# Raw weights of the first column pair loaded before the last expert matrices, into freed token rows, in a fused attention, mixture and feed-forward kernel

## The chip, the cores and the metric

The kernel runs on one core of a Trainium2 chip. The metric is the device time of one execution in microseconds (us), as the median over several runs. Engine names in the profile: PE (TensorE matmul), PEld (TensorE weight load), DVE (VectorE), ACT (ScalarE), POOL (GpSimd), SP (SyncE, which issues all DMAs here; SPq is its queue).

## The reference

Three stages follow each other; all data is float32.

```python
# 1. attention, B=2, H=8, S=768, D=64: keys within 16 of the query, and one summary per block of 32
k_sum = k.reshape(B, H, 24, 32, D).max(axis=3);  v_sum = v.reshape(B, H, 24, 32, D).mean(axis=3)
a = softmax(concat(mask(scale * q @ k.T), scale * q @ k_sum.T + log(32)))
x = (a @ concat(v, v_sum)).reshape(1536, 512)
# 2. soft mixture, 8 experts with 4 slots each, F=1024
logits = x @ phi
slot_in = softmax(logits, axis=0).T @ x                  # "dispatch": 32 slots, 512
slot_out[e] = relu(slot_in[e] @ w1[e]) @ w2[e]           # w1: 8 x 512 x 1024, w2: 8 x 1024 x 512
y = softmax(logits, axis=1) @ slot_out
# 3. feed-forward, 512 -> 2048 -> 512
out = softplus(y @ w_in) @ w_out
```

The inputs are 60 MB, of which w1 and w2 are 16.8 MB each and w_in and w_out 4.2 MB each.

## The kernel before, in words

All work is cut into named tasks (`task`, L171), and two lists written out by hand, `ORDER_A` (L65, attention and dispatch) and `ORDER_B` (L18, experts and feed-forward), say in which order they are emitted (`run`, L174). Each engine executes its own instructions in that order and waits for others by semaphores; so one list sets the order within PE, DVE, ACT, POOL and within the queue of DMA issues on SP. A DMA whose target is still in use holds up all that stand behind it on SP. `warm n` (L650) emits n bf16 filler matmuls on PE.

**Memory.** Ten slots `s0` to `s9` of 16 KB per partition (L138) hold first q, k and v of the four head groups, then w1 (`W1`, L185), then w2 (`W2`, L186: expert 0 in s0, 1 in s1, 2 in the softmax buffer `AB`, 3 to 7 in s6, s7, s8, s9, s2), then the raw words of w_in (s3, s5, s2, s3) and w_out (s4, s6, s9, s4). So w2 of experts 3 to 7 can be sent only when the matmuls that read w1 in that slot are through. The tokens x (the output of attention, `x`, L163) are two tiles of 6 x 512 words per partition; from L657 on their place is given to other pools, among them `wt_p` with two buffers of 4 KB under the tag "wo" and `ep`.

**Attention** (12 steps i of 4 windows, 3 per head group g): `k`, `q`, `v` load; `km` (L251, DVE) takes block maxima; `kf` (L258, POOL) copies keys and maxima into windows; `vp`, `ve` (ACT) copy shifted v rows; `va` to `vd` (PE, ACT) form the block means, and `vf` (`fill_v`, L296, POOL) copies them into rows 96 to 119 of v of both strips (a strip is one of the two alignments of v) for two chunks at once. Then `sc` (PE), `mx`, `sub` (DVE), `ex` (ACT), `tr` (PE), `tc` (ACT), `av` (PE), `dv` (DVE). Dispatch: `xt`, `lt`, `lm`, then `sp` (L474) and `zp` (L518), the last matmuls that read x.

**Experts:** `hu E n` (L785): up projection of experts 2E and 2E+1, half n of the rows of w1, on PE; `hr` (relu, ACT, L796), `ht` (transpose, PE, L801), `hc` (DVE, L806); `dn e h` (L810): down projection of expert e, half h of w2[e], PE; `so` (ACT) collects all but `dn 7 1`, which `yl 0`, `yl 1` (L819) make by themselves; `ya` (L825, DVE) adds, `yt` (PE), `ye` (ACT, DVE) give the transposed slot outputs `soT`. Beside it `c 0` to `c 6`, `ct`, `cc` prepare the combine weights.

**Feed-forward:** w_in and w_out are read as float64-like word pairs and put together: `wia`/`woa` (L712, ACT) rescale the high word, `wib`/`wob` n (n = 0, 1, 2: L718, L720, L723, DVE) shift and merge the fields. They are done in eight pairs p (256 columns of w_in, two rows blocks of w_out); pair 0 is halved (`wia 0 0`, `wia 0 1`). `wh`, `wl` (ACT, DVE) split w_out into a high and a low part. `swc`, `swd`, `swe` (L906, L912, L915) multiply w_in with the slot outputs into `SW`. A visit is 128 columns of the hidden layer for half of the tokens: `ha` (L918, PE), `hx` (softplus, ACT, L931), `hh`, `hl` (high and low part; ACT, DVE), `m` (L943, 18 matmuls per visit into six accumulators); there are 32 visits. `leave` and `out` bring results out.

Loads of raw w_in before: `wi 0 0 0` and `wi 0 0 1` (`load_wi`, L221) are the two column halves of pair 0, all four k, in rows of 1 KB, into s3.

Of the kernel before, what the change touches and what calls it, by code (L numbers as in the profile page):

```python
# [28 lines left out]
m 1 1 1, swd 1:ACT, hl 1, swe 1, wob 1 2, m 1 0 1, woa 2, m 1 1 0, ha 2, m 1 2 1, m 1 0 0, m 1 2 0, wib 2 2, hx 2,  # L29
hh 2, wob 2 0, wh 1, swa 2, m 2 0 0, swb 2:ACT, wia 3, ha 3, hl 2, hx 3, wob 2 1, wl 1:DVE, wob 2 2, hh 3, m 2 0 1,  # L30
m 2 2 1, swc 2, m 2 2 0, m 2 1 1, m 3 0 1, swd 2:DVE, wib 3 0, swe 2, ha 4, wib 3 1, wib 3 2, wo 1 1, wi 2 0, hl 3,
wh 2, woa 3, hx 4, m 2 1 0, m 3 1 1, wob 3 0, wia 4, m 3 0 0, wl 2:DVE, hh 4, swa 3, wib 4 0, swb 3:ACT, m 3 2 1,
ha 5, wo 2 0, swc 3, hl 4, swd 3:ACT, wi 3 1, m 3 1 0, m 4 0 0, hx 5, wo 2 1, m 4 1 0, wob 3 1, m 4 2 1, swe 3,
wob 3 2, woa 5, m 4 1 1, hh 5, ha 6, m 4 2 0, wib 4 1, hl 5, hx 6, m 5 1 1, wh 3, ha 7, hh 6, m 5 0 1, wi 2 1,
m 3 2 0, hx 7, m 6 0 1, ha 8, wia 5, wob 5 0, m 4 0 1, hl 6, hh 7, wib 4 2, m 5 1 0, wl 3:DVE, wia 7, swa 4, hx 8,
m 6 1 1, wib 5 0, swb 4:ACT, m 6 1 0, m 6 0 0, wob 5 1, ha 9, wib 5 1, m 6 2 1, hl 7, m 5 2 1, wi 3 0, wia 6, hx 9,
hh 8, wib 6 0, m 7 4, m 6 2 0, wib 5 2, m 7 3, swc 4, wib 7 0, leave 7 4:ACT, woa 4, m 5 0 0, m 5 2 0, hl 8,
swd 4:ACT, m 7 5, hh 9, wob 5 2, m 7 2, swe 4, ha 10, swa 5, swb 5:ACT, wob 4 0, wib 6 1, wo 3 0, hx 10, wib 7 1,
m 8 4, leave 7 5:DVE, m 7 1, ha 11, wh 5, wob 4 1, leave 7 1:DVE, leave 7 3:DVE, m 7 0, hl 9, wib 6 2, hh 10,
leave 7 0:ACT, m 8 0, swc 5, hl 10, m 8 1, hx 11, m 8 5, leave 7 2:ACT, m 8 2, swd 5:ACT, swe 5, m 8 3, ha 12, swa 6,  # L40
hh 11, wl 5:DVE, m 9 0 1, m 10 1 1, m 11 0 0, woa 6, m 9 1 0, swb 6:ACT, m 10 1 0, hl 11, hx 12, m 9 2 1, m 9 0 0,
ha 13, wob 6 0, m 10 2 1, swc 6, swd 6:DVE, m 11 0 1, wib 7 2, wob 6 1, hx 13, m 10 0 1, m 10 0 0, wob 4 2, m 9 1 1,
wo 3 1, hh 13, m 9 2 0, m 13 0 1, m 13 1 0, swe 6, ha 14, m 11 1 1, swa 7, wh 4, hh 12, m 10 2 0, hl 13, m 13 2 1,
wl 4:DVE, swb 7:ACT, m 11 2 1, hx 14, wob 6 2, ha 15, hl 12, woa 7, m 13 0 0, swc 7, m 12 1 1, m 11 2 0, wob 7 0,
wob 7 1, m 13 1 1, swd 7:DVE, hh 14, m 13 2 0, m 11 1 0, hx 15, hh 15, m 12 2 0, m 12 0 0, m 12 2 1, swe 7, m 14 1 1,
ha 16, m 15 1 1, wh 6, m 14 1 0, hl 15, hx 16, ha 17, m 15 0 0, m 14 0 1, m 12 0 1, m 15 2 1, m 15 0 1, hl 14,
m 15 1 0, hx 17, wob 7 2, hh 16, ha 18, hl 16, m 15 2 0, m 14 0 0, m 12 1 0, hx 18, m 14 2 1, m 16 1 1, m 16 0 1,
hh 17, hl 17, wl 6:DVE, m 16 2 1, m 16 1 0, hh 18, m 16 2 0, ha 19, m 16 0 0, m 17 2 0, hl 18, m 18 0 0, m 17 0 1,
hx 19, ha 20, m 18 2 1, hh 19, m 19 0 1, m 19 1 0, m 17 2 1, hx 20, m 18 1 1, m 18 2 0, m 17 0 0, wh 7, m 14 2 0,
hl 19, m 17 1 0, m 18 1 0, ha 21, m 17 1 1, m 19 1 1, m 19 0 0, hx 21, ha 22, hh 20, m 18 0 1, hl 20, wl 7:DVE,  # L50
m 20 1 0, m 20 0 0, hh 21, hx 22, ha 23, m 20 2 1, m 20 2 0, hh 22, m 21 0 1, m 19 2 0, hl 22, m 22 1 0, m 21 1 0,
m 20 1 1, hl 21, hx 23, ha 24, m 20 0 1, m 21 2 0, m 21 0 0, m 19 2 1, hh 23, hx 24, m 21 1 1, m 22 1 1, ha 25,
m 22 0 1, m 22 2 1, hl 23, hx 25, m 21 2 1, ha 26, m 22 2 0, m 23 4, m 23 5, hh 24, leave 23 5:DVE, m 22 0 0, hl 24,
m 23 2, m 23 1, leave 23 1:DVE, hx 26, m 23 0, hh 25, ha 27, m 23 3, m 24 0, leave 23 4:ACT, m 24 4, m 24 1, hh 26,
hl 25, leave 23 3:DVE, leave 23 2:ACT, m 24 5, m 24 2, hx 27, hl 26, ha 28, leave 23 0:ACT, m 24 3, m 25 1 0,
out 23 1, hh 27, out 23 5, hx 28, m 25 1 1, m 25 0 0, m 25 0 1, hh 28, m 26 1 1, m 25 2 1, hl 28, out 23 4, ha 29,
m 28 0 0, m 26 0 0, m 28 1 0, hx 29, m 28 1 1, m 26 2 1, m 28 0 1, m 27 0 1, m 25 2 0, ha 30, m 28 2 0, m 26 0 1,
m 26 1 0, hl 27, out 23 0, m 26 2 0, hx 30, hh 29, hh 30, m 27 2 0, hl 29, m 29 0 0, m 27 0 0, m 29 1 1, m 27 2 1,
# [7 lines left out]
k 0 0, k 1 0, km 0 0, km 1 0, warm 28, q 0 0, kf 0 0 0:Pool, k 0 1, km 0 1, bias, kf 0 0 1:Pool, kf 1 0 2:Pool, q 0 1,  # L66
kf 0 1 0:Pool, kf 1 0 1:Pool, v 0 0, sc 0, v 0 1, va 0, ve 0 0:ACT, mx 0, k 1 1, q 1 1, sub 0, v 1 0, ve 0 1:ACT,
kf 0 0 2:Pool, kf 0 1 1:Pool, kf 1 0 0:Pool, vb 0:ACT, km 1 1, sc 1, kf 0 1 2:Pool, q 1 0, vp 0 1:ACT, sc 2, ex 0 0,
v 2 0, k 2 0, v 2 1, mx 1, kf 1 1 0:Pool, sub 1, ex 0 1, kf 1 1 1:Pool, vp 0 0:ACT, tr 0 0, tc 0 0:ACT, vc 0, tr 0 1,
vd 0:ACT, vf 0 1:Pool, v 1 1, vf 0 0:Pool, k 2 1, ex 1 0, mx 2, sc 3, sub 2, ex 1 1, tc 0 1:ACT, ve 2 0:ACT, km 2 0,  # L70
tr 1 1, kf 2 0 0:Pool, ex 2 1, tc 1 1:ACT, ex 2 0, vp 1 1:ACT, av 0 0, av 0 1, mx 3, tr 1 0, sc 4, dv 0, tr 2 1, mx 4,
k 3 1, kf 2 0 2:Pool, kf 1 1 2:Pool, tc 1 0:ACT, km 2 1, tc 2 1:ACT, q 2 1, k 3 0, sub 3, va 1, av 1 0, ve 0 2:ACT,
vb 1:ACT, vc 1, ve 2 2:ACT, q 2 0, vp 2 1:ACT, vf 0 2:Pool, w1 3 0, vd 1:ACT, km 3 1, vp 1 0:ACT, kf 2 0 1:Pool,
av 1 1, tr 2 0, ve 2 1:ACT, tc 2 0:DVE, vp 2 0:ACT, ex 3 0, kf 2 1 0:Pool, va 2, kf 2 1 1:Pool, sc 5, phi, ve 1 0:ACT,
vf 1 0:Pool, sub 4, sc 6, dv 1, km 3 0, av 2 1, ex 3 1, mx 5, kf 3 0 0:Pool, av 2 0, ve 1 1:ACT, q 3 1, dv 2, tr 3 0,
vb 2:ACT, ex 4 0, ex 4 1, tr 3 1, sub 5, vf 1 1:Pool, kf 2 1 2:Pool, mx 6, tc 3 0:ACT, w1 1 0, tc 3 1:ACT, vc 2,
ve 1 2:ACT, av 3 1, av 3 0, tr 4 1, kf 3 0 2:Pool, vd 2:ACT, tr 4 0, ex 5 1, sc 7, dv 3, w1 2 1, tc 4 0:ACT, sub 6,
# [949 lines left out]
```

## Time and profile before

| what | us |
|---|---|
| median of 3 runs (290.81 to 291.77) | 290.92 |
| the profiled execution | 291.39 |
| its span in the trace (1.69 lies around it) | 289.7 |
| busy in the span: PE, DVE, ACT, POOL | 274.7, 161.0, 143.1, 33.9 |
| attention and dispatch, to the first up projection | 0 to 85.45 |
| experts, to the last down projection | 85.45 to 119.8 |
| first hidden tile (`ha 0`) | 125.96 |

The times in the trace count from the start of the span. In lists of instructions each line has start, duration, engine, source line, operation, out<-in, count, and in brackets how long the engine was idle before it and what ended that. A run of PE matmuls is pipelined; its pace is read from the starts, not from the durations.

### The profile page before, as it was taken

The numbers are of one execution on the slowest core, as the hardware profiler recorded it, in microseconds if no ns is written. First come the engines' busy times: TensorE is split into PE (matmuls) and PEld (weight loads), VectorE is DVE, ScalarE is ACT, GpSimd is POOL, SyncE is SP. The second block draws the span as 40 slices with busy tenths as digits, with TensorE's granted clock in tenths as the row PEclk, the third lists the DMA queues.
The fourth block names the chain that finished last, engine by engine and source line by source line (L and its number), as shares of the span: only waits on it lengthen the run. The fifth ranks groups of instructions, "written<-read, shape, count | busy, mean of one in ns | idle before, by whom it ended". The sixth has DMA issues, their size and how long they took to land.

```text
span 289.7 us, 5589 instructions
## 1 busy us (share of the span) xinstructions
PE 274.7 (95%) x2340; PEld 191.3 (66%) x2340; DVE 161.0 (56%) x249; ACT 143.1 (49%) x219; POOL 33.9 (12%) x79
## 2 busy tenths in 40 slices
...
DVE  2598978642654030499999999394342221611224
...
GB/s 232 411 409 402 353 417 424 413 425 417 372 292 286 371 422 423 388 399 397 395 395 298 2 1 2 0 0 0 2 0 0 0 2 0 109 111 0 0 0 217
DMA packets 17432, 63.65 MB, mean 220 GB/s; under 512 B 1920, under 2 KB 3072, under 8 KB 13312
## 3 DMA queue, kind: packets, MB, share of 16 engines
...
q8 instruction: 18, 0.29, 0.4%
q14 instruction: 6, 0.05, 0.0%
...
## 4 chain that ended last, share of the span: by engine, by line
PE 57%; DVE 16%; DMA 12%; ACT 8%; issue 4%; SPq 1%; POOL 1%; DVEq 0%; ACTq 0%; POOLq 0%
PE acc L949 36%; DMA wo_raw<-in_moe_w_out 6%; PE av L358 3%; ACT s L166 3%; PE f_ps L923 3%; DMA s<-in_moe_w 3%; PE h_ps L790 3%; DMA s<-in_v 3%; DVE wf L720 2%; DVE gl L768 2%; PE tpa L342 2%; ACT AB L337 2%; DVE wo L720 2%; DVE wf L723 2%; PE tpx L380 2%
## 5 line engine op out<-in xcount | busy, mean ns | idle before, releaser
L949 PE MATMUL acc<-whl,gh 128*128 128x512 f32 x384 | 105.5, 399 | 0.2
L949 PEld LDWEIGHTS acc<-whl,gh 128*128 128x128 f32 x384 | 71.1, 188 | 17.1 <-ACT park L166 0.7
L768 DVE TENSOR_TENSOR gl<-e,gh 128x768 fp32r<-128x768 f32 (+1 forms) x33 | 30.6, 930 | 49.7 <-ACT gh L166 26.3
L949 PE MATMUL acc<-whl,gl 128*128 128x512 f32 x192 | 58.1, 398 | 0.0
L931 ACT ACTIVATE e<-f_ps 128x768 f32<-128x768 f32 (+1 forms) x33 | 26.0, 789 | 42.5 <-PE f_ps L923 21.8
L949 PEld LDWEIGHTS acc<-whl,gl 128*128 128x128 f32 x192 | 35.8, 188 | 8.5 <-DVE gl L768 0.6
L166 ACT ACTIVATE gh<-e 128x768 fp32r<-128x768 f32 (+1 forms) x33 | 27.0, 824 | 24.3 <-PE acc L949 24.0
L166 ACT ACTIVATE s<-s 32x520 f32<-32x520 f32 (+4 forms) x20 | 14.4, 721 | 9.8 <-DMA s<-in_v 9.4
L923 PE MATMUL f_ps<-cs 128*128 128x384 f32 x64 | 16.9, 345 | 1.4 <-DVE cs L768 1.1
L358 PE MATMUL av<-s,AB 120*64 120x65 f32 x384 | 15.7, 226 | 1.3 <-POOL s L249 0.7
L358 PEld LDWEIGHTS av<-s,AB 120*64 120x64 f32 x384 | 13.0, 137 | 5.9 <-issue 3.2
L342 PE MATMUL tpa<-ident,AB 128*120 128x128 f32 x96 | 14.8, 283 | 1.3 <-ACT vs L166 0.5
L249 POOL COPY s<-vs 24x1040 f32<-24x1040 f32 x12 | 12.6, 1053 | 29.3 <-issue 15.3
L923 PEld LDWEIGHTS f_ps<-cs 128*128 128x128 f32 x64 | 11.6, 188 | 5.9 <-DVE cs L768 1.1
L166 ACT ACTIVATE AB<-tpa 120x512 f32<-120x512 f32 x23 | 13.3, 591 | 4.1 <-PE tpa L342 4.0
L325 DVE TENSOR_REDUCE m<-sc 128x8 f32<-128x960 f32 x12 | 13.8, 1150 | 2.5 <-PE sc L320 2.5
L332 DVE TENSOR_TENSOR AB<-sc,m 128x960 f32<-128x960 f32 x12 | 13.8, 1152 | 2.3 <-PE tpa L342 2.1
L337 ACT ACTIVATE AB<-AB 128x480 f32<-128x480 f32 x24 | 13.6, 598 | 1.1 <-DVE AB L332 0.9
L812 PE MATMUL so_ps<-s,hT 128*32 128x512 f32 x104 | 12.4, 597 | 1.8 <-DMA s<-in_moe_w 1.8
L790 PE MATMUL h_ps<-s,siT 128*32 128x512 f32 x128 | 13.9, 593 | 0.0
L342 PEld LDWEIGHTS tpa<-ident,AB 128*120 128x120 f32 x96 | 10.1, 137 | 4.2 <-ACT vs L166 1.2
L320 PE MATMUL sc<-s 64*64 64x120 f32 x384 | 12.1, 263 | 0.5 <-DMA s<-in_q 0.5
(148 smaller groups left out, 310.8 us busy)
## 6 DMA issues: line engine op xcount, KB each, us to landing
s<-in_moe_w SPq DMA_DIRECT2D x30, 1024.0 KB, 12.5
wi_raw<-in_moe_w_in SPq DMA_DIRECT2D x7, 1024.0 KB, 15.3
...
```

Source lines behind the costliest of these rows:

```text
L166: nc.scalar.activation(out=o, in_=i, func=ACTF.Copy)
L249: (nc.vector if eng == "DVE" else nc.gpsimd).tensor_copy(out=o, in_=i)
L325: nc.vector.tensor_reduce(out=m.rearrange("p (e u) -> p e u", e=2), in_=sc_t[i][:, :, 0:480].rearrange("p e (u j) -> p e u j", u=4), axis= ...
L332: nc.vector.tensor_tensor(out=A_t[i], in0=sc_t[i][:, :, 0:480].rearrange("p e (u j) -> p e u j", u=4), in1=m_t[i].rearrange("p (e u) -> p ...
L337: nc.scalar.activation(out=A_t[i][:, e], in_=A_t[i][:, e], func=ACTF.Exp, scale=0.125)
L342: nc.tensor.transpose(tp[0:120, u], A_t[i][:, e, u, :], ident)
L358: mm(out=av_t[i][64 * w:64 * w + 64, e, 65 * u:65 * u + 65], lhsT=AT_t[i][0:120, e, c:c + 64], rhs=v_t[g][0:120, w, 2 * n + t, 2 * a + e, ...
L768: (nc.vector if eng == "DVE" else nc.gpsimd).tensor_tensor(out=o, in0=i, in1=h.bitcast(F32), op=ALU.subtract)
L790: mm(out=h_ps[E][32 * j:32 * j + 32], lhsT=siT[:, kk], rhs=w1_t[2 * E + j // 2, n][:, kk % 2, 512 * (j % 2):512 * (j % 2) + 512], start=(k ...
L923: mm(out=f[n][:, h, 0:384], lhsT=cs_t["SW"][:, J], rhs=cs_t["cS"][:, s0:s0 + 384], **one)
L931: nc.scalar.activation(out=e_[n][:, half(hs)], in_=f[n][:, half(hs), 0:384], func=ACTF.Softplus)
L949: mm(out=acc[(n > 7) + (n > 23), t], lhsT=g, rhs=(wh, wl, wh)[p][J], start=(n in OPEN and p == 0), stop=(n in SHUT and p == 2))
```

## The change

Four edits:
1. `load_wi0` takes the place of `load_wi` for pair 0: `wi 0 0 a` loads k rows 2a and 2a+1 of all 256 columns, in rows of 2 KB, into a tile of `wt_p` with the tag "wo". `wi_parts` cuts pair 0 by k instead of by columns; the instructions of `wia 0 *`, `wib 0 * n` keep their size.
2. `fill_v` copies one strip per call, 24 x 520 words instead of 24 x 1040; there are 24 calls instead of 12.
3. The softmax scalars of `c 0` and `c 2` move to a tile of their own (`cms`), and `cs` grows by 256 words.
4. Both orders are new.

```diff
+    cms = cp.tile([128, 24], F32, name="cms")
...
+    raw0 = {}
+    def load_wi0(a):
+        raw0[a] = wt_p.tile([128, 2, 256, 2], I32, tag="wo", name="raw0")
+        nc.sync.dma_start(
+            out=raw0[a].rearrange("p k f w -> p k (f w)"),
+            in_=w_in.bitcast(I32).rearrange("(k p) f -> p k f", k=4)[:, 2 * a:2 * a + 2, 0:512])
...
-    def fill_v(g, n, eng):
-        o = v_t[g][96:120, :, 2 * n:2 * n + 2].rearrange("p s c h d -> p s c (h d)")
-        m = vs_t[g][96:120].rearrange("p h d -> p (h d)").unsqueeze(1).unsqueeze(1)
-        on(eng, o, m.to_broadcast([24, 2, 2, 260]))
+    def fill_v(g, n, s, eng):
+        o = v_t[g][96:120, s, 2 * n:2 * n + 2].rearrange("p c h d -> p c (h d)")
+        on(eng, o, vs_t[g][96:120].rearrange("p h d -> p (h d)").unsqueeze(1).to_broadcast([24, 2, 260]))
...
-    cs = cs_p.tile([128, 3584], FR, name="cs")
+    cs = cs_p.tile([128, 3840], FR, name="cs")
...
-            t = ep.tile([128, 1560], F32, name="cw")
-            cs_t["m"], cs_t["s"] = t[:, 0:12].unsqueeze(2), t[:, 12:24].unsqueeze(2)
+            t = ep.tile([128, 1536], F32, name="cw")
+            cs_t["m"], cs_t["s"] = cms[:, 0:12].unsqueeze(2), cms[:, 12:24].unsqueeze(2)
...
+        if p == 0:
+            ks = slice(2 * j[0], 2 * j[0] + 2)
+            return wf_t[0][:, ks, 0:256], raw0[j[0]][:, :, :, 1], raw0[j[0]][:, :, :, 0]
...
-            task(("wi", c, h) + j, P(load_wi, c, ("s3", "s5", "s2", "s3")[c], h, *j))
+            task(("wi", c, h) + j, P(load_wi0, *j) if p == 0 else P(load_wi, c, ("s3", "s5", "s2", "s3")[c], h, *j))
```

The start of ORDER_B, to the second visit (`ha 1`) and a little on:

```diff
-warm 2, c 0, hu 1 0, hu 1 1, c 1, hu 0 0, c 2, hu 2 0, hu 2 1, w2 5 0, hu 0 1, c 4, hu 3 0, c 3, hu 3 1, c 6, c 5,
-hr 0, ct 1, w2 5 1, warm 2, w2 7 0, wi 0 0 0, w2 3 0, ht 0, w2 4 0, w2 4 1, warm 2, hr 1, hc 0 1, hc 0 0, ct 0, ht 1,
-hc 1 0, cc 1, dn 0 0, hr 2, ht 2, dn 0 1, hc 2 1, cc 0, hr 3, hc 2 0, ht 3, dn 5 0, w2 6 1, hc 3 0, dn 1 1, wia 0 0,
-w2 6 0, dn 2 0, wib 0 0 0, dn 2 1, hc 1 1, dn 5 1, dn 4 1, hc 3 1, w2 3 1, w2 7 1, dn 4 0, dn 3 0, dn 1 0, dn 6 0,
-dn 3 1, dn 6 1, dn 7 0, wib 0 0 1, wo 0 0 0, yl 1, so, wib 0 0 2, wo 0 0 1, yl 0, woa 0 0, ya 1, wi 0 0 1, woa 0 1,
-warm 2, ya 0, wob 0 0 0, yt 1, wi 0 1, wo 0 1, ct 2, warm 2, yt 0, wob 0 0 1, ye 0:ACT, warm 2, wob 0 1 0, wob 0 0 2,
-fp, warm 2, warm 2, wia 0 1, wob 0 1 1, ye 1:DVE, swc 0 0, wib 0 1 0, wh 0 0, wob 0 1 2, cc 2, swd 0 0:ACT, wib 0 1 1,
-wia 1, warm 2, swe 0 0, warm 2, ha 0, wib 0 1 2, wi 1 0, hx 0 0, wl 0 0:DVE, swc 0 1, wib 1 0, hh 0 0, hl 0 0,
-wib 1 1, hx 0 1, hh 0 1, m 0 0, wh 0 1, m 0 1, hl 0 1, woa 1, m 0 2, wib 1 2, swd 0 1:DVE, wo 1 0, wob 1 0, swe 0 1,
-m 0 3, wl 0 1:DVE, wia 2, swa 1, swb 1:ACT, ha 1, m 0 5, wi 1 1, hx 1, m 0 4, hh 1, swc 1, wib 2 0, wob 1 1, wib 2 1,
+c 0, c 1, warm 2, wi 0 0 1, hu 2 0, hu 2 1, wi 0 0 0, hu 1 0, hu 0 0, hu 0 1, hu 3 0, hr 0, w2 7 0, hu 1 1, warm 2,
+ht 0, warm 2, c 2, warm 2, c 4, hr 1, w2 7 1, hc 0 0, dn 0 0, w2 6 0, ht 1, w2 5 0, dn 0 1, w2 3 1, hu 3 1, wia 0 0,
+warm 2, hc 1 0, warm 2, c 3, hc 0 1, c 5, w2 4 0, w2 4 1, hr 2, wib 0 0 0, w2 5 1, ht 2, c 6, hr 3, dn 2 0, hc 1 1,
+wia 0 1, w2 6 1, hc 2 0, hc 2 1, dn 1 0, ht 3, hc 3 1, ct 0, w2 3 0, dn 5 0, dn 4 0, cc 0, ct 2, wo 0 0 0, dn 1 1,
+warm 2, ct 1, cc 1, hc 3 0, dn 4 1, wib 0 1 0, wo 0 0 1, dn 2 1, dn 5 1, wi 0 1, wib 0 0 1, wib 0 1 1, wi 1 0, dn 6 1,
+dn 6 0, wo 0 1, dn 3 1, wib 0 0 2, dn 3 0, dn 7 0, woa 0 0, yl 0, wib 0 1 2, wob 0 0 0, so, yl 1, wob 0 0 1, ya 0,
+yt 0, warm 2, woa 0 1, ya 1, cc 2, wob 0 1 0, wob 0 0 2, ye 0:ACT, yt 1, fp, wob 0 1 1, wh 0 0, ye 1:DVE, swc 0 0,
+wob 0 1 2, wia 1, wib 1 0, warm 2, warm 2, swd 0 0:ACT, wi 1 1, swe 0 0, ha 0, swc 0 1, wh 0 1, wl 0 0:DVE, hx 0 0,
+hh 0 0, hx 0 1, hh 0 1, wl 0 1:DVE, wo 1 0, wo 1 1, hl 0 0, m 0 2, m 0 0, wib 1 1, wi 2 1, hl 0 1, wia 2, woa 1,
+wib 1 2, m 0 4, m 0 5, swd 0 1:DVE, swe 0 1, swa 1, swb 1:ACT, wob 1 0, ha 1, m 0 1, hx 1, m 0 3, wob 1 1, hh 1,
...
```

The start of ORDER_A (the rest holds the same tasks in another order, with `vf g n s` for `vf g n`):

```diff
-k 0 0, k 1 0, km 0 0, km 1 0, warm 28, q 0 0, kf 0 0 0:Pool, k 0 1, km 0 1, bias, kf 0 0 1:Pool, kf 1 0 2:Pool, q 0 1,
-kf 0 1 0:Pool, kf 1 0 1:Pool, v 0 0, sc 0, v 0 1, va 0, ve 0 0:ACT, mx 0, k 1 1, q 1 1, sub 0, v 1 0, ve 0 1:ACT,
+k 0 1, km 0 1, bias, k 0 0, q 0 1, q 0 0, k 1 0, km 0 0, kf 0 0 2:Pool, v 0 0, kf 0 0 1:Pool, warm 28, ve 0 0:ACT,
+kf 0 0 0:Pool, kf 0 1 1:Pool, km 1 0, sc 1, kf 0 1 0:Pool, vp 0 0:ACT, v 0 1, sc 0, va 0, kf 1 0 1:Pool, k 1 1, q 1 0,
+kf 1 0 0:Pool, q 1 1, mx 1, v 2 0, vb 0:ACT, mx 0, ve 0 2:ACT, kf 0 1 2:Pool, sub 0, vc 0, vd 0:ACT, ex 0 1, sc 2,
...
```

## Rows read from the trace of the kernel before

**Rows 1.** The page's forty slices of the span, 7.24 us each

```profile
DVE  2598978642654030499999999394342221611224
...
GB/s 232 411 409 402 353 417 424 413 425 417 372 292 286 371 422 423 388 399 397 395 395 298 2 1 2 0 0 0 2 0 0 0 2 0 109 111 0 0 0 217
```

**Rows 2.** Busy time by stretch: length, then PE, PEld, DVE, ACT, POOL, granted clock, DMA

```profile
12.00:24.00 12.00, 10.97 (x221) 7.68 (x223) 11.32 (x15) 11.35 (x19) 6.90 (x17) 1.00 1.04 414
24.00:36.00 12.00, 10.79 (x208) 7.86 (x210) 11.06 (x21) 10.84 (x20) 8.60 (x17) 1.00 0.98 367
...
84.50:88.40 3.90, 3.90 (x46) 1.45 (x48) 2.62 (x7) 1.81 (x2) 0.00 (x0) 1.00 0.13 44
88.40:99.40 11.00, 11.00 (x105) 3.20 (x98) 1.77 (x5) 0.69 (x1) 0.00 (x0) 1.00 0.95 352
99.40:118.70 19.30, 17.55 (x148) 6.36 (x152) 2.86 (x11) 3.71 (x6) 0.00 (x0) 1.00 1.01 420
...
127.70:180.00 52.30, 50.98 (x299) 37.21 (x302) 51.80 (x62) 38.34 (x52) 0.00 (x0) 1.00 0.59 226
180.00:284.70 104.70, 104.70 (x484) 84.52 (x476) 37.56 (x43) 38.60 (x50) 0.00 (x0) 1.00 0.05 20
```

**Rows 3.** The chain that ended last, 85 to 122 us: start, duration, what

```profile
85.52 8.77 PE h_ps L790 x80
...
94.73 8.96 DMA s<-in_moe_w
...
103.71 17.55 DMA wo_raw<-in_moe_w_out
```

**Rows 4.** The lists of waits of SP's queue and of POOL: total, times, longest

```profile
SPq L217 <- PE h_ps L790: 16.8, 3, 12.5
...
POOL hT L780 <- PE s_ps L518: 0.8, 1, 0.8
```

**Rows 5.** Instructions in order of time, last down projections and what follows on PE

```profile
112.30 0.13 PEld L812 LDWEIGHTS so_ps<-s,hT 128*32 128x32 f32 x4 [0.30 <-issue]
113.67 0.16 PEld L812 LDWEIGHTS so_ps<-s,hT 128*32 128x32 f32 x8 [1.24 <-DMA s<-in_moe_w]
116.16 0.16 PEld L812 LDWEIGHTS so_ps<-s,hT 128*32 128x32 f32 x8 [2.33 <-DMA s<-in_moe_w]
...
118.66 0.67 PEld L823 LDWEIGHTS so_ps<-s,hT 128*32 128x32 f32 x16 [0.62 <-DMA s<-in_moe_w]
...
120.62 0.47 PEld L702 LDWEIGHTS ct_ps<-ident,cw 128*128 128x128 f32 x4
...
121.90 1.02 PEld L653 LDWEIGHTS <-warm_x 128*128 128x128 bf16 x6
```

**Rows 6.** Instructions in order of time, from the sum of slot outputs to the second visit

```profile
119.70 0.76 DVE L827 TENSOR_TENSOR so<-so_ps,so 128x256 f32<-128x256 f32 x2 [12.06 <-ACT so L166]
...
120.62 0.43 DVE L718 TENSOR_SCALAR wo<-wo 128x512 int32<-128x512 int32 x1 [0.16 <-ACT wo L712]
...
121.08 0.69 DVE L720 SCALAR_TENSOR_TENSOR wo<-wo_raw,wo 128x512 int32<-128x512 int32 x1
...
125.37 1.13 ACT L712 ACTIVATE wf<-wi_raw 128x1024 f32<-128x1024 f32 x1 [0.34 <-DMA wi_raw<-in_moe_w_in]
...
125.96 0.59 PE L923 MATMUL f_ps<-cs 128*128 128x384 f32 x2 [0.43 <-DVE cs L768]
...
126.46 0.68 DVE L768 TENSOR_TENSOR whl<-wo,whl 128x512 fp32r<-128x512 f32 x1
...
127.06 0.68 DVE L718 TENSOR_SCALAR wf<-wf 128x1024 int32<-128x1024 int32 x1
...
132.42 0.59 PE L923 MATMUL f_ps<-cs 128*128 128x384 f32 x2 [0.69 <-DVE cs L768]
```

**Rows 7.** POOL's copies by shape: count, busy us, mean ns

```profile
L249 POOL COPY s<-vs 24x1040 f32<-24x1040 f32 x12 | 12.6, 1053 | 29.3 <-issue 15.3 <-PE av L358 13.7
L249 POOL COPY s<-s 128x384 f32<-128x384 f32 x24 | 12.1, 505 | 2.7 <-DMA s<-in_k 2.4
```

More of the change, by code (lines that the diff above doesn't have):

```diff
@@ L29 @@
[L29 to L58, printed above, removed]
@@ new lines @@
+yt 0, warm 2, woa 0 1, ya 1, cc 2, wob 0 1 0, wob 0 0 2, ye 0:ACT, yt 1, fp, wob 0 1 1, wh 0 0, ye 1:DVE, swc 0 0,
+wob 0 1 2, wia 1, wib 1 0, warm 2, warm 2, swd 0 0:ACT, wi 1 1, swe 0 0, ha 0, swc 0 1, wh 0 1, wl 0 0:DVE, hx 0 0,
+hh 0 0, hx 0 1, hh 0 1, wl 0 1:DVE, wo 1 0, wo 1 1, hl 0 0, m 0 2, m 0 0, wib 1 1, wi 2 1, hl 0 1, wia 2, woa 1,
+wib 1 2, m 0 4, m 0 5, swd 0 1:DVE, swe 0 1, swa 1, swb 1:ACT, wob 1 0, ha 1, m 0 1, hx 1, m 0 3, wob 1 1, hh 1,
+wib 2 0, swc 1, wob 1 2, wib 2 1, m 1 1 1, m 1 1 0, m 1 0 1, wo 2 1, swd 1:ACT, swe 1, hl 1, woa 2, wob 2 0, wi 2 0,
```

95 lines of the change are left out of this document (62 added, 33 removed).

## The prediction

> **What bounds the kernel now.** I read the slices first [rows 1]. The DMA engines carry 353 to 425 GB/s from the second slice to the 21st, with one dent in slices 12 and 13 (292, 286). DVE is full in slices 18 to 25. The busy times by stretch [rows 2] split this into stages. From 12 to 36 us ACT and DVE are nearly full (22.2 and 22.4 of 24 us). From 127.7 to 180 DVE is full (51.8 of 52.3), with PE only 1.3 us short of it (50.98). From 180 on PE alone is (104.7 of 104.7): each us by which the matmuls of the feed-forward stage begin earlier, and stay supplied, ends the kernel a us earlier. [...]
>
> The dent is a hole. From 84.5 to 88.4 us the queue carries 44 GB/s, from 88.4 to 99.4 it carries 352, then 420 [rows 2]. The queue's own waits name the cause [rows 4]: three loads of w2 (L217) stand 16.8 us in all behind the up projections, whose slots they go into. The chain [rows 3] shows what the hole costs: up projections, then w2 landing, then raw w_out landing at 121.25, then DVE work. PE feels it too: before the last four of 15 down projections it waits for w2 twice [rows 5]. Four weight loads take 0.13 + 0.30 = 0.43 us with the pause behind them, so the group at 112.30 is through at 112.73, the next starts at 113.67 (0.94 lost); that one lasts 0.86, and the next starts at 116.16 (1.63 lost). That is 2.57 us.
>
> **The hole filled.** `wi 0 0 1` and `wi 0 0 0` (0.52 MB each) no longer go into s3, which wants `hu 2 0` and `hu 2 1`, but into `wt_p`, on the place of x. The last readers of x are the `zp` matmuls; POOL's clearing of hT, which also lies there, waits for just those (L518) [rows 4] and starts at 83.02. So the two loads are issued near 83 and move 1.05 MB by 420 GB/s = 2.5 us into the hole. Bounds: at 82.3 they cost nothing; issued at 85 or later, they push the first w2 by up to 1.5 us. I take 83. On SP they now stand in front of all w2 of ORDER_B; none of those can go before the first up projection ends near 87.2, so nothing queued behind loses.
>
> The up projections are reordered with them: `hu 2 0` first, which frees `w2 7 0` at 87.2; `w2 7 1` at 88.9; `w2 6 0` and `w2 5 0` at 90.7 (one `hu` is 16 of the 80 matmuls that take 8.77 us, so 1.75 us [rows 3]). Four MB are then in the queue before it can run dry, and the other six follow by 98. Ten w2 are 10.5 MB: from 88.4 at 420 GB/s they end at 113.4, where before they and 0.5 MB of w_in ended at 118.66 [rows 5]. The 16 DMA engines don't end together; I allow 1.5 us and take 115. `dn 3 0`, the one that reads the last load, comes up on PE near 116. So the 2.57 us of waits go. Bounds: all, or, if the rate stays 352 GB/s, none (a rival, below).
>
> The trace carries 420 GB/s from 99.4 to 118.7 [rows 2]. [...]
>
> **What PE gets in addition.** Between the first up projection and `yl` the new order has six pairs of fillers where the old had two: 8 fillers of 0.2 us (six weight loads 1.02 us apart in all) [rows 5] = +1.6. `ct 2` moves in front of `yl`: +0.47 [rows 5]. With the waits gone, the end of `yl` moves by -2.57 + 1.6 + 0.47 = **-0.5 us**. PE is then without a gap there; what is late next is PE itself, not a load.
>
> **DVE behind `yl`.** DVE idles before 119.70 and has no pause after it [rows 6]. Between `ya` and the sum that lets `ha 0` start, the old order has `wob 0 0 0`, `wob 0 0 1`, `wib 0 1 0`, `wib 0 1 1` which the new has before `ya` (0.43 + 0.69 + 0.43 + 0.69 = 2.24) [rows 6]; it can, because the raw words are there 2.5 us or more earlier. The new one puts `wib 1 0` in (0.68) [rows 6]. Net **-1.55**. From there to `ha 1` the old has `wib 0 1 2` (0.69), `wib 1 0` (0.68) and `wob 1 0` (0.68), the new `wl 0 1` (0.68) instead: **-1.37**. `ha 1` starts at 132.42, 6.46 after `ha 0`, and its last wait is for DVE [rows 6], so this counts. Against it: `woa 0 0` needs `wo 0 0 0`, which I see landing at 117 to 118, so `wob 0 0 1` (0.69) may still run when `ya 0` wants DVE; I give back **+0.4**.
>
> **Costs taken at nothing.** The 24 half copies on POOL: by a line through 505 ns for 384 words and 1053 for 1040 [rows 7] one takes 0.62, so +2.3 us of POOL in all. POOL is busy 15.5 of 24 us where it is fullest [rows 2], which covers it; if not, `av` waits, and bounds are -0.7 (the half that is ready lets it start early) to +0.7. `cms` and the wider `cs` add no instruction. Pair 0 cut by k keeps the instruction sizes; `swc 0 0` now needs both halves, done long before. `woa 0 0` takes a buffer that `wib 0 0 2` has left; both stand in that order on DVE and ACT before `so`, covered by the down projections. The new order of attention has the same instructions; PE loses 2.2 us in 12 to 36 us, with DVE and ACT full, so I see little to gain: 0, bounds -1 and +1. The order after `ha 1`: 0, bounds -0.8 and +0.8, since PE is at 51 of 52.3 us already.
>
> **Sum:** -0.5 - 1.55 - 1.37 + 0.4 = -3.0 us. On the profiled execution's 291.39 that is 288.4; the median of the runs stands 0.47 below it, so 290.92 - 3.0 = **287.9**.
>
> **Rivals.** (a) *w2 arrives no sooner.* The stream stays at 352 GB/s, as from 88.4 to 99.4 [rows 2]: ten w2 then end at 118.2, `dn 3 0` and `dn 7 0` follow, and `yl` ends 1.6 us later than I say. Then DVE runs out of work ahead of `ya`, and 0.5 of its gain goes as well: -0.9, 290.0. For it: PE-side waits were by arrival; against it: 420 in the next stretch, and SP's waits explain the 352. [...] (b) *Slower: the first pair waits for the second.* The new order puts `wia 1` ahead of `swd 0 0` on ACT and `wib 1 0` ahead of `swe 0 0` on DVE. Both need `wi 0 1`, which before was awaited at 125.37 [rows 6]. If it lands no earlier, then 1.13 (`wia 1`), 0.28 (`swd`), 0.68 and 0.29 follow and `ha 0` starts near 127.7, 1.7 later than now; `ha 1` gets 1.37 back and the rest of the stage has its DVE work no sooner: +0.4 to +1.7, middle 292.0. It decides from a landing at 122.3 on; I see it at 120 to 121, since 1 MB less stands in front of it after the hole and `wi 0 0 1` is no longer there. (c) *The attention order gives the gain back:* DVE now takes the block maximum of `k 1 0` before the first score maximum, and 12 to 36 us is DVE's and ACT's stage; 2 to 3 us lost there leaves 290.5 or so, no change. For it: two full engines; against it: the amount of work is the same.
>
> **Numbers.** A measurement of this kernel can tell 0.3% (0.9 us) from no change. Forecast 0.64, by its bounds 286.2 (attention -1, later order -0.7) to 289.8; (a) 0.14, half of it beyond 0.9 us; (b) 0.12; (c) 0.10, of which 0.02 slower. Faster 0.71, same 0.15, slower 0.14. The range 286.2 to 291.0 takes in the forecast, (a) and most of (c).
>
> **What would show it.** Right: no stretch under 200 GB/s between 83 and 99 us; no wait of L812 for a DMA over 0.3 us; `yl` near 118.8, `ha 0` near 123.4 and `ha 1` near 129.4 with the first up projection still at 85.4; PE full until the end. Wrong: ACT waiting for raw w_in ahead of `swd 0 0` (b); L812 still waiting (a); the first up projection later than 86 (c); or `ha 1` early by 3 us and the gain gone by 180, which no case here holds.

## The result and the profile after

The kernel after takes **283.80 us** (median of 4 runs, 283.69 to 284.62) against 291.04 of the kernel before beside it (4 runs, 290.81 to 291.77): ratio 0.9753, 95% interval 0.9728 to 0.9779. That is 7.2 us faster. Forecast were 3.0 us, 287.9, and a range down to 286.2; the time lies below the range.

The profiled execution of after took 284.62 us, its span is 282.9. By stage, from the starts in both traces (the collecting copy is ACT's `so`, which begins when all down projections but `dn 7 1` are through):

| stretch, us | before | after | difference | predicted |
|---|---|---|---|---|
| start to the first up projection | 85.45 | 81.44 | -4.01 | 0 |
| to the collecting copy | 33.62 | 35.95 | +2.33 | -0.5 |
| to `ha 0` | 6.89 | 5.53 | -1.36 | -1.15 (-1.55 + 0.4) |
| to `ha 1` | 6.46 | 6.16 | -0.30 | -1.37 |
| to the start of the last `m` | 153.26 | 149.80 | -3.46 | 0 |
| to the end | 4.00 | 4.01 | +0.01 | 0 |

`ha 1` starts 3.34 us earlier, close to the 3.0 forecast, but by other terms, so the nearness is luck; and the rest of the gain comes where none was seen.

The first two rows vary from one execution to the next. In a second profiled execution of the same kernel (the one with `ha 0` at 122.66, below) they are 82.22 and 34.93, so -3.2 and +1.3; their sum, -1.7 and -1.9, is steadier. Over all profiled runs the first up projection starts at 84.84 to 85.48 with the old order of attention, and at 81.13 to 82.22 with the new order and its half copies.

The slices of after (GB/s), which answer to [rows 1]:

```profile
GB/s 211 401 398 395 408 417 409 417 421 418 416 410 411 423 415 416 392 399 400 387 402 177 3 0 0 2 0 2 0 0 0 0 2 0 8 178 2 0 58 202
```

Busy time by stretch of after, columns and stretches as in [rows 2], with one stretch of attention more; then that stretch before:

```profile
24.00:36.00 12.00, 11.42 (x226) 8.71 (x226) 11.38 (x21) 11.05 (x21) 10.41 (x26) 1.00 1.03 399
48.00:60.00 12.00, 11.59 (x203) 8.78 (x199) 7.12 (x17) 9.73 (x18) 3.46 (x6) 1.00 1.01 416
...
84.50:88.40 3.90, 3.90 (x44) 1.21 (x40) 0.45 (x2) 0.00 (x0) 0.00 (x0) 1.00 1.05 405
88.40:99.40 11.00, 11.00 (x98) 3.58 (x90) 1.80 (x7) 2.65 (x4) 0.00 (x0) 1.00 1.01 417
99.40:118.70 19.30, 17.21 (x150) 6.30 (x146) 5.15 (x15) 4.47 (x8) 0.00 (x0) 1.00 1.02 409
127.70:180.00 52.30, 51.47 (x312) 38.46 (x311) 50.33 (x59) 37.16 (x50) 0.00 (x0) 1.00 0.48 182
```

```profile
48.00:60.00 12.00, 10.94 (x189) 7.89 (x187) 7.04 (x14) 9.55 (x19) 1.05 (x1) 1.00 1.02 419
```

The hole is gone, as forecast: 405 and 417 GB/s where [rows 2] have 44 and 352. PE is busier from 24 to 36 us (11.42 for 10.79) and from 48 to 60 (11.59 for 10.94), which the prediction took as unchanged. And in attention the stream is no faster than before but a little slower: slices 2 to 11 have 395 to 421 GB/s, where [rows 1] have 402 to 425 but for two (353 and 372).

PE still waits for w2. Weight loads in order of time, after, which answer to [rows 5]:

```profile
105.19 0.16 PEld L825 LDWEIGHTS so_ps<-s,hT 128*32 128x32 f32 x8 [1.16 <-DMA s<-in_moe_w]
...
110.19 0.40 PEld L825 LDWEIGHTS so_ps<-s,hT 128*32 128x32 f32 x8 [0.46 <-DMA s<-in_moe_w]
112.75 0.19 PEld L825 LDWEIGHTS so_ps<-s,hT 128*32 128x32 f32 x8 [2.15 <-issue]
...
115.20 0.30 PEld L825 LDWEIGHTS so_ps<-s,hT 128*32 128x32 f32 x8 [0.56 <-DMA s<-in_moe_w]
```

Where nothing is late, these rows have 0.17 or 0.30 of idle time; here are 1.16 and 2.15. The trace puts the 2.15 down to `issue`, but a load of w2 lands at 112.64, just ahead of 112.75, so it is a wait for w2 too. The up projections begin 4.0 us earlier, the last w2 lands 3.45 earlier (115.16 for 118.61), and the stretch to the collecting copy grows by 2.3.

From the collecting copy to `ha 1`, after, in order of time, which answers to [rows 6]:

```profile
117.39 0.60 ACT L169 ACTIVATE so<-so_ps 128x512 f32<-128x512 f32 x1 [0.15 <-PE so_ps L825]
...
118.34 0.75 DVE L840 TENSOR_TENSOR so<-so_ps,so 128x256 f32<-128x256 f32 x2
...
120.60 1.13 ACT L722 ACTIVATE wf<-wi_raw 128x1024 f32<-128x1024 f32 x1
...
122.48 0.29 DVE L781 TENSOR_TENSOR cs<-sw_ps,cs 64x128 fp32r<-64x128 f32 x1
122.81 1.29 DVE L781 TENSOR_TENSOR whl<-wo,whl 128x512 fp32r<-128x512 f32 x2
...
122.92 0.59 PE L936 MATMUL f_ps<-cs 128*128 128x384 f32 x2
...
124.69 0.56 DVE L781 TENSOR_TENSOR gl<-e,gh 128x384 fp32r<-128x384 f32 x1 [0.58 <-ACT gh L169]
...
129.08 0.62 PE L936 MATMUL f_ps<-cs 128*128 128x384 f32 x2 [0.40 <-ACT swg L169]
```

DVE has less to do between `ya` and `ha 0`, as forecast. Behind `ha 0` it now idles 0.58 us, until ACT has made the high part of the first softplus: that was not.

The matmuls of `m` (PE's 576 accumulating matmuls) at 211 to 222 us, where PE has nothing but them and `ha`; durations in ns, least, median, most. Before, then after:

```profile
L949 PE MATMUL acc<-whl,gh x29: 391/394/400, 211.1 to 221.9; 128*128 128x512 f32 x29
```

```profile
L962 PE MATMUL acc<-whl,gh x33: 389/389/398, 210.9 to 221.2; 128*128 128x512 f32 x33
```

The same matmul, same size, granted clock 1.00 in both, is 5 ns shorter. From start to start of two that follow each other the mean is 234.0 ns before (517 pairs) and 228.8 after (515): 576 x 5.2 = 3.0 us of the 3.46 in the table.

### The profile page after: what moved, and what is told of

The parts are those of the page before. It is cut to its first block, busy times and chain, and to the rows that moved or that the text cites. A ratio compares the mean times of both kernels' runs of the same rounds, so it can differ in the third digit from the quotient of the medians.

```text
span 282.9 us, 5606 instructions
## 1 busy us (share of the span) xinstructions
PE 270.5 (96%) x2340; PEld 190.5 (67%) x2340; DVE 161.7 (57%) x249; ACT 143.7 (51%) x219; POOL 35.3 (12%) x91
## 4 chain that ended last, share of the span: by engine, by line
PE 71%; DVE 9%; ACT 8%; DMA 8%; issue 2%; POOL 1%; SPq 0%; ACTq 0%; DVEq 0%; POOLq 0%
PE acc L962 41%; DMA wo_raw<-in_moe_w_out 6%; PE h_ps L803 5%; PE f_ps L936 4%; PE tpa L351 3%; PE av L367 3%; ACT s L169 2%; PE sc L329 2%; ACT AB L346 2%; PE tpx L389 2%; DMA s<-in_k 2%; ACT AB L169 2%; DVE wf L730 1%; DVE wf L733 1%; DVE gl L781 1%
## 5 line engine op out<-in xcount | busy, mean ns | idle before, releaser
L962 PE MATMUL acc<-whl,gh 128*128 128x512 f32 x384 | 103.6, 394 | 0.3 <-ACT gh L169 0.3
L962 PE MATMUL acc<-whl,gl 128*128 128x512 f32 x192 | 56.6, 394 | 0.0
L261 POOL COPY s<-vs 24x520 f32<-24x520 f32 x24 | 14.0, 619 | 15.5 <-ACT vs L169 15.1
L367 PE MATMUL av<-s,AB 120*64 120x65 f32 x384 | 14.7, 226 | 0.0
L825 PE MATMUL so_ps<-s,hT 128*32 128x512 f32 x104 | 13.0, 598 | 1.5 <-DMA s<-in_moe_w 1.5
L722 ACT ACTIVATE wo<-wo_raw 128x1024 f32<-128x1024 f32 (+1 forms) x9 | 9.4, 1040 | 7.7 <-DMA wo_raw<-in_moe_w_out 7.1
```

The source lines that it names most:

```text
L261: (nc.vector if eng == "DVE" else nc.gpsimd).tensor_copy(out=o, in_=i)
L367: mm(out=av_t[i][64 * w:64 * w + 64, e, 65 * u:65 * u + 65], lhsT=AT_t[i][0:120, e, c:c + 64], rhs=v_t[g][0:120, w, 2 * n + t, 2 * a + e, ...
L962: mm(out=acc[(n > 7) + (n > 23), t], lhsT=g, rhs=(wh, wl, wh)[p][J], start=(n in OPEN and p == 0), stop=(n in SHUT and p == 2))
```

## Experiments

Theory after the two traces: the gain has three parts, the new order of attention, the prediction's own terms in experts and feed-forward, and the *place* of tiles in memory. The new tile `cms` of 96 bytes stands ahead of the ten slots, so every slot moves by 96 bytes, and with them the split words of w_out, `whl`, that the `m` matmuls stream. Rival: all of it is the orders. Medians are in us; "hu" is the start of the first up projection; pace is the mean from start to start as above.

**Place alone.** The kernel before, with a tile that nothing uses:

```diff
     rs = cp.tile([128, 1], F32, name="rs")
+    pad = cp.tile([128, 24], F32, name="pad")
```

> The kernel before with one unused tile of 96 bytes, as large as the tile for the softmax scalars in the change; every slot, and with them the split w_out that the last matmuls stream, lies 96 bytes higher; order and loads are those of before. Theory place: the pace of the 576 matmuls of 128x512 depends on where w_out lies against the activations (64-byte phase 0 before, 32 in the changed kernel); start to start falls from 234 to 228 or 227 ns, 576 x 5 to 6 ns = 3.0 to 3.7 us, the time is 287 to 288 us. Rival order: the faster pace comes from the new order of matmuls; here it stays at 234 ns and the time at 291.0, within 0.5 us.

289.16 (10 runs) against 291.34, ratio 0.9915 (0.9884 to 0.9946). Pace 228.6. With 16 words in place of 24 (64 bytes):

> The same with 64 bytes, so that the 64-byte phase of w_out stays 0 while its address moves. Theory place by 64-byte phase: pace 234 ns, 291.0 us within 0.5. Rival: any other address than the old one will do (phase in 128 bytes or more); pace 228 ns, 287 to 288 us. Rival order: 234 ns, 291.0.

291.23, ratio 0.9986 (0.9953 to 1.0019), pace 233.1. The page's groups, 96 bytes, then 64 (busy us, mean ns):

```profile
L950 PE MATMUL acc<-whl,gh 128*128 128x512 f32 x384 | 103.5, 394 | 0.5 <-ACT park L167 0.2
```

```profile
L950 PE MATMUL acc<-whl,gh 128*128 128x512 f32 x384 | 105.2, 399 | 0.2
```

So the place alone is worth about 2 us (2.2, by the interval 1.6 to 3.4) in a kernel whose orders are untouched, and the rival falls for this part. The time still missed the 287 to 288 of the theory, since `ha 0` came 0.6 later with the 96 bytes (126.58); the next runs say why.

**The kernel after with the slots back on multiples of 64 bytes** (of 256, as it turned out):

```diff
-    cms = cp.tile([128, 24], F32, name="cms")
+    cms = cp.tile([128, 32], F32, name="cms")
...
-    cs = cs_p.tile([128, 3840], FR, name="cs")
+    cs = cs_p.tile([128, 3832], FR, name="cs")
```

> The changed kernel with the scalars' tile widened from 96 to 128 bytes (and the tile of combine weights narrowed by 32 to keep the rest in place): w_out goes back to phase 0, all else is the changed kernel. Theory place: pace 234 ns, 3.0 us more than the changed kernel, 286.8 us. Rival order: 227 to 229 ns and 283.8 us.

284.66, ratio 0.9773 (0.9705 to 0.9841). Pace 233.2: lost again, as the theory has it. But the time is not its 286.8: `ha 0` starts at 121.09, 1.8 earlier than in after; the loads run at 422 to 425 GB/s from 36 to 72 us (after: 413 to 419), and no down projection waits. What the slots' place gives the matmuls it takes from the loads. The kernel after, unchanged, beside others, tells whether that is chance:

> The kernel after, unchanged, beside the others on one chip. If the place of the slots slows the loads: the first hidden tile comes at 122.5 to 123.2 us again, loads at 413 to 417 GB/s from 36 to 72 us, 283.8 us. If it was the run or the chip: near 121.1 us with 422 to 425 GB/s, 282 to 283 us.

284.20, ratio 0.976 (0.9725 to 0.9795); `ha 0` at 122.66, 411 to 419 GB/s from 36 to 72. So it is not the run. Over all profiled runs the mean from 36 to 72 us goes with the place of the slots modulo 256 bytes: 421 to 424 GB/s at 0 (four runs), 418 to 421 at 128 (five), 416 at 192 (one), 415 to 416 at 224 (five). To have both, only `whl` was moved, 32 bytes into its four slots:

```diff
-            whl[b] = wp.tile([128, 2, 4, 512], FR, tag=("s1", "s7", "s8", "s9")[b], name="whl")
+            t = wp.tile([128, 4112], FR, tag=("s1", "s7", "s8", "s9")[b], name="whl")
+            whl[b] = t[:, 8:4104].rearrange("p (i j d) -> p i j d", i=2, j=4)
```

> The kernel after, with the ten slots on multiples of 64 bytes again (as before), and w_out's split words alone 32 bytes further in their slots. Theory (the accumulating matmuls go faster when the words they stream lie 32 bytes off a multiple of 64, and the loads go slower when their target does): matmuls of the feed-forward start 228 to 229 ns apart, as after, and the first hidden tile comes near 121.1 us, as in the run with all on multiples of 64, so that the time is 281.8 to 282.6 us. Rival one (the loads' rate only varies from run to run): first hidden tile near 122.9, 283.8 us. Rival two (the place of other buffers made the matmuls faster): 233 ns apart, 284.7 us.

284.66, ratio 0.9773 (0.9736 to 0.9809). Neither side: pace 231.1, and by slot 230.4, 232.3, 233.1, 228.7. The slots had grown by 64 bytes each, so the four places differ modulo 256: 32, 96, 160, 224. In after all four are at 224, before at 128. With all slots on multiples of 256, and `whl` 224 bytes into its own (`t[:, 56:4152]`):

> The kernel after, all ten slots on multiples of 256 bytes (as in the run with all on multiples of 64, where the loads ran at 422 to 425 GB/s), and w_out's split words 224 bytes into their slots (the remainder modulo 256 that they have in the kernel after). Theory (the streamed words' place sets the pace of the matmuls by a finer remainder than 64, and the slots' place sets the loads' rate): matmuls 228 to 229 ns apart in all four slots of split words, first hidden tile at 121.0 to 121.5 us, 281.6 to 282.4 us. Rival one (the pace hangs on something else than the place of these words): 231 to 233 ns, 284 us or more. Rival two (loads vary by run): first hidden tile near 122.8, 283.8 us.

**282.18**, ratio 0.9685 (0.9648 to 0.9722), faster than both kernels. Slices and group of its page, then `ha 0`:

```profile
GB/s 217 410 413 412 418 426 419 423 426 426 427 404 375 426 426 421 407 417 414 405 421 92 1 0 2 0 0 2 0 0 0 0 2 0 25 162 2 0 63 199
...
L963 PE MATMUL acc<-whl,gh 128*128 128x512 f32 x384 | 103.6, 394 | 0.3 <-ACT gh L169 0.3
```

```profile
120.37 0.59 PE L937 MATMUL f_ps<-cs 128*128 128x384 f32 x2
```

Pace 228.8 and loads of 422 to 426 GB/s together. The same kernel with `whl` at 224, 32, 64 and 16 in its four slots (one execution):

> The placed version, with the four slots of split words at four remainders modulo 256 bytes: 224 (row blocks 0 to 3), 32 (4 to 7), 64 (8 to 11), 16 (12 to 15). Known from the runs: 0, 64-multiples and 96, 160 give 232 to 234 ns, 224 gives 227 to 229. If nearness to a multiple of 256 on either side, but not on it, makes the matmuls fast: 32 gives 228 to 229 and 64 gives 233. If 224 alone does: 32 and 64 both 233. What 16 gives is open. Time between 282.2 and 283.8 us by how many are fast.

284.08, above the range, and neither theory holds. Pace by place modulo 256, in ns, from several runs (slots 2 and 3 are used when DVE and ACT are quieter, in after 36.0 and 37.1 of the 98 us from 180 on, for 50.3 and 37.2 of the 52.3 ahead of that; there 224 gives 227.5 to 228.7; earlier, it gives 228.7 to 229.1 in slot 1 and 230.7 to 231.6 in slot 0):

```
 0: 233.1 233.5 233.2 (slots 1 to 3)      16: 231.4 (slot 3)     32: 230.4 (slot 0), 230.2 (slot 1)
64: 234.0 (slot 2)   96: 232.3 (slot 1)  128: 234.1 234.2 (slots 2, 3)  160: 233.1 (slot 2)
192: 233.2 233.1 (slots 2, 3)            224: 228.1 227.6 (slots 2, 3)
```

224 is fast; 32 is as fast in slot 0 and 1.1 to 1.5 ns slower in slot 1; 16 lies half way; the others are slow. Why is open. In every kernel here `gh` and `gl`, the words that PE loads as weights for these matmuls, lie at 224 too. So no run tells whether 224 itself counts, or lying at the same remainder as they do.

**Attention alone.** The kernel before with the ORDER_A of after, and its `fill_v` by strips:

> The kernel before with only the new attention order and the half copies it is written for; experts, loads of raw weights, places and the second order as before. The first up projection started 4.0 us earlier in the changed kernel. Theory attention: it does so here (81.4 us). What comes of it: if the experts wait for w2 that is sent behind the hole, whose start moves with the up projections, the last w2 lands some 2 to 4 us earlier too and the time is 287 to 289; rival stream: DMA has carried all it could up to 80 us, the last w2 lands at most 1.5 us earlier, and the time is 289.5 to 291.

288.08, ratio 0.9862 (0.9799 to 0.9926); hu at 81.53, `ha 0` at 122.64, pace 234.0. The chain of waits, which answers to [rows 3]:

```profile
81.60 8.77 PE h_ps L790 x80
91.17 9.25 DMA s<-in_moe_w
100.44 17.49 DMA wo_raw<-in_moe_w_out
```

The same chain, 3.3 to 3.9 us earlier: order A by itself moves all that follows. Is it the order or the halves? The halves at their places in the order of before:

```diff
-vd 0:ACT, vf 0 1:Pool, v 1 1, vf 0 0:Pool, ...
+vd 0:ACT, vf 0 1 0:Pool, vf 0 1 1:Pool, v 1 1, vf 0 0 0:Pool, vf 0 0 1:Pool, ...
```

> The kernel before with each copy of block means cut into one per strip, at the same places of the order. Theory (the order gives attention its 4 us): first up projection at 85.2 to 85.7 us, 291.2 us, within 0.3%. Rival (a half that is ready lets its matmuls start): first up projection at 84.5 us or earlier, 290.3 us or less. Other rival (2.3 us more on POOL delay the values): 86.1 us, 292 us.

291.39, ratio 1.0 (0.9969 to 1.0031); hu at 85.11. The halves alone give nothing beyond the 0.6 by which runs with the old order differ among themselves. The new order with whole copies, each where its first half was (`vf 0 2:Pool` for `vf 0 2 1:Pool`, the second half left out of the list):

> The kernel before with the new order of attention, but with the block means copied for both strips in one instruction, at the place where the new order has the first half. If the order alone makes attention faster: first up projection at 81.3 to 81.8 us, 288.1 us, as with the halves. If the halves are needed for it (a half on POOL of 0.62 us lets its matmuls start earlier than a whole of 1.05): first up projection at 82.5 us or later, 289.0 us or more.

290.52 (10 runs, 288.03 to 291.41), ratio 0.997 (0.994 to 1.0); hu at 82.83. So in this order the halves are worth some 1.3 us, and the order the other 2.6 (one trace each). POOL's copies in order of time and the first value matmuls on PE show it; whole copies, then halves (the run with attention alone):

```profile
15.47 1.05 POOL L249 COPY s<-vs 24x1040 f32<-24x1040 f32 x1
17.68 2.17 POOL L249 COPY s<-vs 24x1040 f32<-24x1040 f32 x2 [1.16 <-ACT s L166]
22.04 1.15 PE L358 MATMUL av<-s,AB 120*64 120x65 f32 x32
```

```profile
15.85 1.75 POOL L251 COPY s<-vs 24x520 f32<-24x520 f32 x3
20.76 1.15 PE L357 MATMUL av<-s,AB 120*64 120x65 f32 x32
```

With whole copies ACT waits 1.15 us until POOL is through with the first, and POOL's next waits 1.16 until ACT has written the other strip; the first value matmuls start at 22.04 for 20.76. The time tells less than hu, because six of these ten executions have a mean granted clock of 0.991 to 0.994 (290.17 to 291.41 us; the other four, at 0.998 to 1.000, 288.03 to 289.99); where the profiled one lost it stands in the last section.

**Without the new attention.** The kernel after with the ORDER_A of before:

> The kernel after with the old order of attention and dispatch (block means still copied per strip). If the prediction's sum is right and attention, experts and place add up: the first hidden tile near 123.4 and the second near 129.4 us with the first up projection at 85.4, and 285.3 us (3.0 from the experts, 2.7 from the place). If the stream of loads bounds everything up to the last expert, so that the raw words only trade places with w2: the first hidden tile at 124 to 125.5 us, 286.5 to 287.5 us. If raw loads and the new order of the experts give nothing by themselves: 288.5 us.

286.35, ratio 0.9833 (0.9791 to 0.9874); hu 85.48, `ha 0` 124.71, `ha 1` 130.86, pace as in after. No down projection waits. Then the same with every slot at its old place modulo 256 (`cms` of 64 words), so that only the prediction's own terms are left:

> The kernel after with the old order of attention and dispatch, and with 256 bytes for the softmax scalars' tile, so that every slot keeps the remainder modulo 256 that it had before: what is left of the change is the raw loads, the new order of experts and feed-forward and the split copies, which is what the prediction's sum is for. Prediction's sum: first hidden tile at 123.9 to 124.4, second at 129.4, 288.0 us. By the run with the old attention order in the new place: no wait for w2, first hidden tile at 124.5 to 124.8, second at 130.7 to 131.0, matmuls 233 to 234 ns apart, 288.9 to 289.4 us. Rival (without the new attention this change gives nothing): 290.5 us or more.

288.67, ratio 0.9907 (0.987 to 0.9944): **-2.65 us, where the prediction's sum says -3.0**; the terms below show that they come near each other by luck. First up projection at 84.86 (0.6 earlier), collecting copy at 118.88, pace 234.1, last `m` 2.8 us earlier than before. The two hidden tiles:

```profile
124.27 0.59 PE L934 MATMUL f_ps<-cs 128*128 128x384 f32 x2
...
130.43 0.62 PE L934 MATMUL f_ps<-cs 128*128 128x384 f32 x2 [0.40 <-ACT swg L167]
```

**The raw loads late.** After, with `wi 0 0 1` and `wi 0 0 0` behind the first two w2 in the list:

```diff
-c 0, c 1, warm 2, wi 0 0 1, hu 2 0, hu 2 1, wi 0 0 0, hu 1 0, ... w2 7 0, hu 1 1, ... hr 1, w2 7 1, hc 0 0,
+c 0, c 1, warm 2, hu 2 0, hu 2 1, hu 1 0, ... w2 7 0, hu 1 1, ... hr 1, w2 7 1, wi 0 0 1, wi 0 0 0, hc 0 0,
```

> The kernel after, with the two loads of raw w_in issued behind the first two w2 instead of ahead of all ten; nothing else. If the raw loads fill a hole of the stream: no load can be issued from the last load of the dispatch until the first up projections end at 83.4, the stream falls under 250 GB/s around 80 to 84 us, every w2 lands some 2 us later, the first hidden tile comes at 124.5 to 125.5, 285.6 to 286.6 us. If the new order of attention keeps the stream full anyway: no hole, first hidden tile near 122.8, 283.9 us.

284.73, ratio 0.9774 (0.9737 to 0.9811); after has 283.80 and 284.20. The hole shows, as stretches of 78 to 96 us:

```profile
78.00:84.00 6.00, 6.00 (x76) 3.27 (x80) 4.21 (x14) 1.68 (x2) 1.14 (x2) 1.00 0.94 389
84.00:90.00 6.00, 6.00 (x64) 1.81 (x60) 0.83 (x2) 0.13 (x1) 0.00 (x0) 1.00 0.88 326
90.00:96.00 6.00, 6.00 (x54) 1.98 (x46) 0.19 (x1) 1.37 (x2) 0.00 (x0) 1.00 1.04 416
```

After has 414, 405 and 421 there, 0.65 MB more, 1.6 us of the stream. But the last w2 lands only 0.2 later (115.34 for 115.16) and `ha 0` 0.2 to 0.5 (123.11). The edit that names the change is worth 0.5 to 0.9 us; why the rest of the 1.6 did not reach `ha 0` was not found out.

**Fewer fillers.** The placed kernel, 282.18, without four of its six pairs in the experts (the `warm 2` on both sides of `c 2`, ahead of `hc 1 0` and ahead of `ct 1`):

> The run before this one, without four of the filler pairs between the first up projection and the last down projection (two remain, as in the kernel before). If PE sets the end of the experts there (its down projections follow each other without a wait): the prediction's price, 1.6 us less, first hidden tile near 119.6, 280.2 us. If w2's arrival is as near as PE: the waits of the down projections take the fillers' place, first hidden tile at 120.6 to 121.2 us, 281.3 to 281.9 us. If the clock falls without them: granted clock below 1.00 in the experts, slower.

282.20, ratio 0.9681 (0.9638 to 0.9724); the clock stays at 1.00. The waits for w2 take their place: 1.2 us in four waits, and a pause of 1.7, where the placed kernel has 0.6 in all. The fillers cost nothing here.

## Why the prediction was wrong

**The hole** was read rightly: it closed, its cause was the queue's wait for up projections. With the old attention, the case that the prediction reckoned with, it only shrinks: the run with old attention and old place has 263 GB/s from 84.5 to 88.4 and 387 from there to 99.4, for 44 and 352 before, and its last w2 lands at 116.5, not at 115. Wrong was when the raw loads go: they were issued at 77.3 and 77.7 (80.6 and 81.0 in that run), not 83: SP's queue waited 6.5 us for the matmuls of `sp` (L474 before, L483 after), not for those of `zp`. That was harmless.

**"-0.5 to the end of the down projections"** came at +0.4 without the new attention (old place): 34.02 against 33.62, with no w2 late. By the starts on PE the down projections take 1.86 us less there, not 2.57, the fillers 1.74 more and the transposes of `ct` 0.56 more. In the kernel after it is +2.3 (+1.3 in its second execution), by two causes that the prediction had not: the up projections come sooner than w2 follows (4.0 us for 3.45), and with the slots' new place the stream is slower (413 to 419 GB/s from 36 to 72 us, for 422 to 425 in the run with the slots back on multiples of 256). With the slots there it is 34.02 again (115.86 - 81.84 and 115.15 - 81.13).

**"Net -1.55, given back +0.4" on DVE** was right, in its parts too: -1.36 in all, where DVE's stretch from `ya` to the sum ahead of `ha 0` shrinks by 1.68 (4.14 for 5.82) and `ya` comes 0.32 later behind the collecting copy; in the run with old attention and old place it is -1.50 (5.39 for 6.89). The two pauses of DVE before (0.16 and 0.22) were overlooked, but are small.

**"-1.37 from `ha 0` to `ha 1`"** failed. It summed DVE's instructions, as if nothing but DVE set this stretch. But `gl` of the first tile starts 1.77 us after `ha 0` before (127.73 - 125.96, by the trace of before, where DVE reaches it without a pause) and 1.77 after (124.69 - 122.92, where it waits for softplus and the high part on ACT): the DVE work that left the stretch ahead of it left a pause of 0.58. Behind `gl`, DVE's sum ahead of `ha 1` comes 0.60 sooner (3.65 us after `gl` for 4.25), but `ha 1` then waits for `swb 1` on ACT (the last row above, 0.40). What counted was 0.3.

**"The later order: 0, bounds ±0.8"** came at -0.8: from `ha 1` to the last `m` the run with old attention and old place has 152.48 for 153.26. So the terms that the prediction added up to -3.0 were measured at -1.4 (+0.4 - 1.5 - 0.3). The -2.65 of that run has besides these the -0.8 of the later order and -0.6 ahead of the first up projection, both put at 0; the -0.6 is no more than what runs with the old attention differ by among themselves.

**"The new order of attention has the same instructions ...: 0, bounds -1 and +1"** is the step that failed by most: -4.0 at the first up projection, -3.3 in the time. The prediction looked at busy time of DVE and ACT from 12 to 36 us and saw them full; but PE idles there and up to the end of dispatch, and the idle time could go. PE's idle time ahead of the first up projection (neither a matmul nor a weight load) is 7.4 us before and 4.7 in the run with attention alone, so 2.7 of its 3.9 us; where the other 1.2 come from was not taken apart. From 12 to 36 us, the stage that the prediction looked at, the kernel after has 0.5 us more of busy PE; from 36 to 72 it has 1.2 more (35.11 for 33.91), and there DVE and ACT are not full before (21.3 and 26.2 of 36 us). Same instructions in another order is no reason for zero where no engine is full from end to end. Part of it could also have been priced from the waits on that path, with what releases each. Before, from 12 to 36 us, PE's weight loads have this row, and none like it in the run with the new order:

```profile
PEld av L358 <- POOL s L249: 1.5, 3, 0.5
```

**"`cms` and the wider `cs` add no instruction"** was the second large miss: they cost no instruction, and moved every slot by 96 bytes. Worth 2.1 to 2.3 us where the stream is not the bound (286.35 against 288.67), and 0.5 to 0.9 in the kernel after (against 284.66, whose four runs spread from 284.12 to 287.40), since the faster matmuls (228.8 ns for 233.2) are partly paid for by slower loads (`ha 0` at 122.92 and 122.66 for 121.09). No row of before can show this; the diff's new tile ahead of the slots was the one hint, and it was read for instructions only.

The parts alone make -3.26 (attention) - 2.65 - 2.18 (place) = -8.1; together they make -7.2. What is missing, 0.9, fits the waits for w2 behind the +2.3 of the experts, which the run with the old attention has not. **The rivals:** (a) was near in kind, w2 late for PE, but by an earlier start, with a stream only 1 to 2% slower; (b) did not come, `wia 1` runs at 120.60 without a wait; (c) had the sign wrong.

The prediction took 420 GB/s for the stream: after has 405 to 417 from 84.5 to 118.7 us, the placed kernel 418 to 427 in eleven slices. From 36 to 72 us the runs have 421 to 424 GB/s with the slots on multiples of 256 bytes, 418 to 421 at 128 and 415 to 416 at 224, so about 1 and 2% less by the place; what sets this was not shown. (w_in and w_out are float64 and 8.4 MB each, not 4.2 as the section on the reference has it; only so do the inputs make 60 MB.)
